# A sketched attention and a Fourier mixer in one kernel: q features made transposed on array tiles, rows s and s+544 folded, one written order

## The chip, the cores and the metric

The kernel runs on 1 core of one Trainium2 chip. The metric is device time in microseconds (us) from one launch to its end. The kernel before took 225.29 us, the median of three runs (224.28 to 231.45). The engines named here are TensorE (PE, with its weight loads as PEld), VectorE (DVE), ScalarE (ACT), GpSimd (POOL) and SyncE (SP, which only issues transfers here).

## The reference

```python
# q, k, v: (4, 4, 1088, 32) = (B, H, S, D); S1, S2: (8, 32); w_ch1 (128, 512); w_ch2 (512, 128)
def phi(x):                                   # 64 features for a row of 32
    a = einsum('rd,bhsd->bhsr', S1, x)
    b = einsum('rd,bhsd->bhsr', S2, x)
    return einsum('bhsi,bhsj->bhsij', a, b).reshape(*x.shape[:-1], 64)
kv  = einsum('bhsf,bhsd->bhfd', phi(k), v)
z   = sum(phi(k), axis=2)
x   = einsum('bhsf,bhfd->bhsd', phi(q), kv) / (einsum('bhsf,bhf->bhs', phi(q), z) + 1e-6)
x   = x.transpose(0, 2, 1, 3).reshape(B, S, 128)
u   = x + real(fft(fft(x, axis=1), axis=2))   # 1088 points along the rows, 128 along the columns
un  = (u - mean(u, -1)) / sqrt(var(u, -1) + 1e-6)
out = u + maximum(un @ w_ch1, 0) @ w_ch2      # (4, 1088, 128) float32
```

## The kernel before

Rows go in 9 tiles of a batch: 8 of 128 rows and one of 64. The type is float32 up to x and bfloat16 behind it. There are two halves.

**Attention, one batch at a time** (loop at L201). Twelve transfers bring q, k, v of the batch, in pieces of 128 bytes, half of q and k from ACT's queue, the rest from SP's (L208-L223). PE transposes q and k, tile by tile, with an identity (`ptr`, L255), ACT copies the result out (L261). `pab` (L269) multiplies the transposed rows by a block matrix of S1 and S2, which gives a and b of all four heads, row by row; ACT copies them (`ab`, L277), and DVE (two tiles of three) or POOL (the third) multiplies a by b into the 256 features of a row (`pp`, L282). So the features have rows in partitions. For k that is what the next product needs: `pkvz` (L292) sums features times [v, 1] over the 9 tiles, for two heads at a time, and ACT puts the two diagonal blocks into `kvz_sb` (L296, L297). For q it isn't: PE transposes the features once more (`pqpt`, L307), ACT copies them (`qpt_sb`, L315), `pnd` (L319) multiplies them by `kvz_sb`, and DVE divides, in three instructions for each tile and pair of heads (`recip` L327, `x_all` L329 and L336).

**Fourier and mixer.** A table of cosines and sines, 1088 rows by 545 columns, is made on DVE and ACT, tile by tile (`trig_tables`, L110 to L126), four tiles at the start and five behind batch 0. `emit_stage_a_main` (L154) multiplies x by it: for each batch 18 products of 512 columns and 18 of 33 (`za`, `za2`, `zbb`), which ACT copies into `zc`, `zs` and `zsn` (minus `zs`). Columns beyond 544 come from symmetry: DVE makes reversed copies (`zcr`, `zsr`, L379, L380). The last loop (L373 on) goes tile by tile: `pu` (L454 to L456) sums cosine part, sine part and x itself; DVE takes mean and variance, ACT the root, DVE normalises (`un`, L467), ACT copies u out (L471), PE transposes `un` (L475), and for four tiles at a time `ph` (L411), relu on ACT or DVE (L419, L422), `po` (L427), an addition of u on DVE (L435) and a store of 128 rows from SP's queue. 48 products of zeros (`wburst`, L383), 16 (`warm1`, L240) and 6 in float32 (`warm`, L230) are there to hold TensorE's clock and belong to no result.

**The order.** The code is written stage by stage. A scheduler of the framework places each engine's instructions, so products of different batches stand mixed on PE. Waits come from tile pools: a tile is handed out again when its last reader is done. In the last loop, tile 4 holds rows of both halves of the spectrum: for it the nested function `u_groups` writes output rows 0-31, 32-63 and 64-127 by three products each, group after group.

Of the kernel before, what the change touches and what calls it, by code (L numbers as in the profile page):

```python
# [42 lines left out]
def kernel(  # L43
# [35 lines left out]
    wdummy = const.tile([128, 512], BF16, name="wdummy")
    nc.gpsimd.memset(wdummy[:], 0.0)  # L80

    bias_negpi = const.tile([128, 1], FP32, name="bias_negpi")
    nc.vector.memset(bias_negpi[:], float(-np.pi))
    bias_eps = const.tile([128, 1], FP32, name="bias_eps")
    nc.vector.memset(bias_eps[:], 1e-6)

    s12 = const.tile([16, 32], FP32, name="s12")
    nc.sync.dma_start(s12[0:8, :], S1[:, :])
    nc.sync.dma_start(s12[8:16, :], S2[:, :])
    sblk = const.tile([128, 4, 16], FP32, name="sblk")  # L90
    nc.gpsimd.memset(sblk[:], 0.0)
    with tc.tile_pool(name="cps", bufs=1, space=bass.MemoryType.PSUM) as cps:
        ps12 = cps.tile([32, 16], FP32, name="ps12")
        nc.tensor.transpose(ps12[:, :], s12[:, :], ident_f[0:16, 0:16])
        for h in range(H):
            nc.vector.tensor_copy(sblk[32 * h : 32 * h + 32, h, :], ps12[:, :])

    kk_i = const.tile([128, KHALF], I32, name="kk_i")
    nc.gpsimd.iota(kk_i[:], pattern=[[1, KHALF]], base=0, channel_multiplier=0)
    kk_f = const.tile([128, KHALF], FP32, name="kk_f")  # L100
    nc.vector.tensor_copy(kk_f[:], kk_i[:])
    s_i = const.tile([128, NT], I32, name="s_i")
    nc.gpsimd.iota(s_i[:], pattern=[[128, NT]], base=0, channel_multiplier=1)
    s_f = const.tile([128, NT], FP32, name="s_f")
    nc.vector.tensor_copy(s_f[:], s_i[:])

    MAGIC = float(1.5 * (2 ** 23))
    TWOPI = float(2.0 * np.pi)

    def trig_tables(out_cos, out_sin, kq_ap, s_scalar_ap, ncols, tagsuf):  # L110
        x = const.tile([128, ncols], FP32, name="tx", tag="tx" + tagsuf)
        nc.vector.tensor_scalar(out=x[:], in0=kq_ap, scalar1=s_scalar_ap, scalar2=None,
                                op0=MULT)
        xc = const.tile([128, ncols], FP32, name="txc", tag="txc" + tagsuf)
        nc.vector.tensor_scalar(out=xc[:], in0=kq_ap, scalar1=s_scalar_ap, scalar2=0.25,
                                op0=MULT, op1=ADD)
        u = const.tile([128, ncols], FP32, name="tu", tag="tu" + tagsuf)
        nc.vector.tensor_scalar(out=u[:], in0=x[:], scalar1=MAGIC, scalar2=MAGIC,
                                op0=ADD, op1=SUB)
        uc = const.tile([128, ncols], FP32, name="tuc", tag="tuc" + tagsuf)  # L120
        nc.vector.tensor_scalar(out=uc[:], in0=xc[:], scalar1=MAGIC, scalar2=MAGIC,
                                op0=ADD, op1=SUB)
        nc.vector.tensor_tensor(out=x[:], in0=x[:], in1=u[:], op=SUB)
        nc.vector.tensor_tensor(out=xc[:], in0=xc[:], in1=uc[:], op=SUB)
        nc.scalar.activation(out=out_sin, in_=x[:], func=ACT.Sin, scale=TWOPI)
        nc.scalar.activation(out=out_cos, in_=xc[:], func=ACT.Sin, scale=TWOPI)  # L126

    kkq_d = const.tile([128, 128], FP32, name="kkq_d")
    nc.vector.tensor_scalar(out=kkq_d[:], in0=kk_f[:, 0:128], scalar1=1.0 / 128.0,
                            scalar2=None, op0=MULT)  # L130
    cd_b = const.tile([128, 128], BF16, name="cd_b")
    sd_b = const.tile([128, 128], BF16, name="sd_b")
    trig_tables(cd_b[:, :], sd_b[:, :], kkq_d[:, :], s_f[:, 0:1], 128, "d")

    kkq_s = const.tile([128, KHALF], FP32, name="kkq_s")
    nc.vector.tensor_scalar(out=kkq_s[:], in0=kk_f[:, :], scalar1=1.0 / S,
                            scalar2=None, op0=MULT)
    cst_b = const.tile([128, NT, KHALF], BF16, name="cst_b")
    sst_b = const.tile([128, NT, KHALF], BF16, name="sst_b")

    def emit_strig(t):
        trig_tables(cst_b[:, t, :], sst_b[:, t, :], kkq_s[:, :], s_f[:, t : t + 1],
                    KHALF, "s")

    for t in (0, 1, 2, 3):
        emit_strig(t)

    z_pool = ctx.enter_context(tc.tile_pool(name="zsb", bufs=B))
    ps_za = ctx.enter_context(tc.tile_pool(name="ps_za", bufs=1, space=bass.MemoryType.PSUM))
    zcs = [None] * B  # L150
    zss = [None] * B
    zsns = [None] * B

    def emit_stage_a_main(b):  # L154
        zc = z_pool.tile([128, KHALF], BF16, name="zc", tag="zc")
        zs = z_pool.tile([128, KHALF], BF16, name="zs", tag="zs")
        zsn = z_pool.tile([128, KHALF], BF16, name="zsn", tag="zsn")
        za = ps_za.tile([128, 512], FP32, name="za", tag="za")
        for t in range(NT):
            rows = rows_of_tile(t)  # L160
            nc.tensor.matmul(za[:, :], x_all[0:rows, b, t, :], cst_b[0:rows, t, 0:512],  # L161
                             start=(t == 0), stop=(t == NT - 1))
        nc.scalar.copy(zc[:, 0:512], za[:, :])
        za2 = ps_za.tile([128, 512], FP32, name="za2", tag="za")
        for t in range(NT):
            rows = rows_of_tile(t)
            nc.tensor.matmul(za2[:, :], x_all[0:rows, b, t, :], sst_b[0:rows, t, 0:512],
                             start=(t == 0), stop=(t == NT - 1))
        nc.scalar.copy(zs[:, 0:512], za2[:, :])
        nc.scalar.mul(zsn[:, 0:512], za2[:, :], -1.0)  # L170
        zbb = ps_za.tile([128, 512], FP32, name="zbb", tag="za")
        for t in range(NT):
            rows = rows_of_tile(t)
            nc.tensor.matmul(zbb[:, 0:33], x_all[0:rows, b, t, :], cst_b[0:rows, t, 512:KHALF],
                             start=(t == 0), stop=(t == NT - 1))
        for t in range(NT):
            rows = rows_of_tile(t)
            nc.tensor.matmul(zbb[:, 64:97], x_all[0:rows, b, t, :], sst_b[0:rows, t, 512:KHALF],
                             start=(t == 0), stop=(t == NT - 1))
        nc.scalar.copy(zc[:, 512:KHALF], zbb[:, 0:33])  # L180
        nc.scalar.copy(zs[:, 512:KHALF], zbb[:, 64:97])
        nc.scalar.mul(zsn[:, 512:KHALF], zbb[:, 64:97], -1.0)
        zcs[b] = zc
        zss[b] = zs
        zsns[b] = zsn

    with ExitStack() as aph:
        qin_pool = aph.enter_context(tc.tile_pool(name="qin", bufs=2))
        vin_pool = aph.enter_context(tc.tile_pool(name="vin", bufs=2))
# [11 lines left out]
        for b in range(B):  # L201
            if b >= 2:
                emit_stage_a_main(b - 2)
# [169 lines left out]
    for b in range(B):  # L373
# [139 lines left out]
```

## Time and profile before

| What | us |
|---|---|
| median of three runs | 225.29 (224.28 to 231.45) |
| the profiled execution: its span, first to last instruction | 224.3 |
| its own time (the lowest of the three runs, equal to the span) | 224.28 |
| ScalarE busy | 91.0 |
| GpSimd busy | 20.6 |
| mean granted TensorE clock | 0.794 of full |
| bytes moved | 10.04 MB in 61571 packets, 56560 of them under 512 B |

Busy times are sums over the whole span and overlap between engines. A matmul's own time holds its way through the array (0.22 us for 128 columns of bfloat16), so the distance from one start to the next, not the duration, tells what a product costs in a dense run. A float32 product is recorded as two matmuls with a weight load each.

### The profile page before, as it was taken

How to read it: one execution, taken by the hardware profiler on the slowest of the kernel's cores; microseconds unless marked ns; L12 is line 12 of the kernel's file. 1: busy time of each engine (PE TensorE's matmuls, PEld its weight loads, DVE VectorE, ACT ScalarE, POOL GpSimd, SP SyncE). 2: the span in 40 equal slices, each digit the busy share in tenths (PEclk: the TensorE clock that was granted, in tenths of full speed). 3: DMA queues.
4: the chain of work that ended last, by engine and by line, in shares of the span. 5: the costliest groups of instructions: out<-in, count | busy, mean ns of one | idle time of the engine just before them, and what ended most of it. 6: DMA issues, size and time to landing. Idle time of an engine off the chain costs nothing.

```text
span 224.3 us, 3592 instructions
## 1 busy us (share of the span) xinstructions
PE 185.6 (83%) x1157; PEld 128.2 (57%) x1157; DVE 138.3 (62%) x549; ACT 91.0 (41%) x290; POOL 20.6 (9%) x46
## 2 busy tenths in 40 slices
PE   0491599988848999999999999898999867868872
PEld 0231466878535978788879876553655433434431
DVE  2034897569995312668474456745387886877751
ACT  0030655357535321453252143514364464545440
POOL 3000131200031200132203100000000000000000
PEclk9997557999965555899995599959999996785555
DMA  8999995049800002400000000000011011111011
GB/s 102 142 130 194 164 151 56 4 73 155 87 0 0 0 0 43 65 0 3 1 0 0 3 1 1 3 0 0 21 29 53 26 38 42 35 34 33 24 36 41
DMA packets 61571, 10.04 MB, mean 45 GB/s; under 512 B 56560, under 2 KB 61424, under 8 KB 61552
## 3 DMA queue, kind: packets, MB, share of 16 engines
q1 hardware_dynamic: 42288, 6.95, 23.3%
q10 hardware_dynamic: 19264, 2.87, 10.6%
q8 instruction: 9, 0.15, 0.3%
q14 instruction: 10, 0.08, 0.1%
HBM read 7.58 MB, written 2.23 MB: 44 GB/s over the span
## 4 chain that ended last, share of the span: by engine, by line
PE 67%; DVE 12%; ACT 8%; ACTq 5%; DMA 4%; issue 2%; DVEq 0%
PE pkvz L292 9%; PE pab L269 9%; PE pnd L319 8%; PE pqpt L307 6%; ACTq L217 5%; PE wburst L383 5%; PE ph L411 5%; PE po L427 5%; DMA w_f<-in_moe_w_ch_dram 4%; PE za L161 4%; PE ptr L255 3%; ACT ht L419 2%; PE warm_621 L240 2%; PE pu L454 2%; PE put L475 2%
## 5 line engine op out<-in xcount | busy, mean ns | idle before, releaser
L327 DVE RECIPROCAL recip<-pnd 128x2 f32<-128x2 f32 (+1 forms) x72 | 12.0, 167 | 33.2 <-PE pnd L319 32.5
L319 PE MATMUL pnd<-kvz_sb,qpt_sb 128*128 128x66 f32 x144 | 29.8, 299 | 0.7 <-DVE recip L327 0.5
L319 PEld LDWEIGHTS pnd<-kvz_sb,qpt_sb 128*128 128x128 f32 x144 | 25.0, 215 | 7.2 <-issue 1.2
L282 DVE TENSOR_TENSOR pp<-ab 128x256 f32<-128x256 f32 (+1 forms) x48 | 21.2, 456 | 8.9 <-ACT ab L277 8.8
L292 PE MATMUL pkvz<-vin,pp 128*128 128x66 f32 x144 | 25.6, 317 | 0.0
L292 PEld LDWEIGHTS pkvz<-vin,pp 128*128 128x128 f32 x144 | 23.4, 232 | 2.0 <-issue 0.5
L427 PE MATMUL po<-w_b,ht 128*128 128x128 bf16 (+1 forms) x144 | 20.1, 251 | 4.3 <-DVE ot L435 3.6
L282 POOL TENSOR_TENSOR pp<-ab 128x256 f32<-128x256 f32 x24 | 17.2, 721 | 57.3 <-ACT ab L277 57.3
L307 PE MATMUL pqpt<-ident_f,pp 128*128 128x128 f32 (+1 forms) x72 | 19.1, 335 | 3.3 <-DVE pp L282 2.9
L427 PEld LDWEIGHTS <-ht 128*128 128x128 bf16 (+1 forms) x144 | 12.4, 111 | 15.3 <-issue 9.9
L277 ACT COPY ab<-pab 128x64 f32<-128x64 f32 (+1 forms) x72 | 13.9, 216 | 16.3 <-PE pab L269 15.4
L411 PE MATMUL ph<-unT,w_b 128*128 128x512 bf16 (+1 forms) x48 | 16.5, 387 | 4.4 <-ACT ht L419 2.2
L329 DVE TENSOR_SCALAR x_all<-pnd,recip 128x32 bf16<-128x32 f32 (+1 forms) x72 | 17.5, 242 | 0.4
L315 ACT COPY qpt_sb<-pqpt 128x512 f32<-128x512 f32 (+1 forms) x24 | 11.1, 463 | 15.7 <-PE pnd L319 9.5
L336 DVE TENSOR_SCALAR x_all<-pnd,recip 128x32 bf16<-128x32 f32 (+1 forms) x72 | 17.3, 240 | 0.0
L161 PE MATMUL za<-cst_b,x_all 128*128 128x512 bf16 (+1 forms) x36 | 16.2, 453 | 0.8 <-DVE x_all L336 0.8
L422 DVE TENSOR_SCALAR ht<-ph 128x512 bf16<-128x512 f32 (+1 forms) x24 | 12.8, 533 | 5.5 <-PE ph L411 4.9
L307 PEld LDWEIGHTS pqpt<-ident_f,pp 128*128 128x128 f32 (+1 forms) x72 | 12.3, 194 | 6.8 <-DVE pp L282 3.7
L435 DVE TENSOR_TENSOR ot<-po,u_sb 128x128 f32<-128x128 f32 (+1 forms) x36 | 10.3, 286 | 8.9 <-PE po L427 8.3
L269 PE MATMUL pab<-sblk,kT 128*128 128x64 f32 (+1 forms) x72 | 15.7, 340 | 0.0
L419 ACT ACTIVATE ht<-ph 128x512 bf16<-128x512 f32 (+1 forms) x24 | 11.3, 472 | 9.3 <-PE ph L411 9.2
L269 PEld LDWEIGHTS pab<-sblk,kT 128*128 128x128 f32 (+1 forms) x72 | 13.9, 252 | 1.7 <-ACT qpt_sb L315 0.4
(98 smaller groups left out, 325.8 us busy)
## 6 DMA issues: line engine op xcount, KB each, us to landing
vin<-in_v_dram SPq DMA_DIRECT2D x15, 144.0 KB, 4.0
out_dram<-ot SPq DMA_DIRECT2D x32, 64.0 KB, 1.5
qin<-in_q_dram SPq DMA_DIRECT2D x8, 144.0 KB, 5.8
kin<-in_k_dram SPq DMA_DIRECT2D x8, 144.0 KB, 4.1
qin<-in_q_dram ACTq DMA_DIRECT2D x7, 144.0 KB, 4.5
kin<-in_k_dram ACTq DMA_DIRECT2D x7, 144.0 KB, 6.3
w_f<-in_moe_w_ch_dram ACTq DMA_DIRECT2D x2, 256.0 KB, 6.7
qin<-in_q_dram ACTq DMA_DIRECT2D x1, 128.0 KB, 5.1
```

Of the source, the lines that this page charges most:

```text
L161: nc.tensor.matmul(za[:, :], x_all[0:rows, b, t, :], cst_b[0:rows, t, 0:512], start=(t == 0), stop=(t == NT - 1))
L269: nc.tensor.matmul(pab[0:rows, :, :], srcT[:, 128 * t : 128 * t + rows], sblk[:, :, :], start=True, stop=True,)
L277: nc.scalar.copy(ab[0:rows, :, :], pab[0:rows, :, :])
L282: eng.tensor_tensor(out=pp[0:rows, :, :, :], in0=in0, in1=in1, op=MULT)
L292: nc.tensor.matmul(pkvz[:, :, :], lhsT, rhs, start=(t == 0), stop=(t == NT - 1))
L307: nc.tensor.transpose(pqpt[:, col : col + rows], qp_tiles[t][0:rows, h0 : h0 + 2, :, :], ident_f[0:rows, 0:rows],)
L319: nc.tensor.matmul(pnd[0:rows, :, :], qpt_sb[:, c0 : c0 + rows], kvz_sb[:, :, :], start=True, stop=True,)
L329: nc.vector.tensor_scalar(out=x_all[0:rows, b, t, (h0 + 0) * D : (h0 + 1) * D], in0=pnd[0:rows, 0, 0:D], scalar1=recip[0:rows, 0:1], scala ...
L336: nc.vector.tensor_scalar(out=x_all[0:rows, b, t, (h0 + 1) * D : (h0 + 2) * D], in0=pnd[0:rows, 1, 0:D], scalar1=recip[0:rows, 1:2], scala ...
L411: nc.tensor.matmul(ph[:, 0:group_rows], w1_b[:, 128 * c : 128 * c + 128], unT[:, 0:group_rows], start=True, stop=True,)
L419: nc.scalar.activation(out=ht[:, c, 0:group_rows], in_=ph[:, 0:group_rows], func=ACT.Relu)
L427: nc.tensor.matmul(po[0:rows, :], ht[:, c, colbase : colbase + rows], w2_b[:, c, :], start=(c == 0), stop=(c == 3),)
```

## The change

All stages are written anew as named steps with an engine, a function that issues them, and a place in one long string that gives the issue order of all engines; a second string gives each step's PSUM bank. Nothing else orders the work: each engine takes its own steps in that order, with waits for what they read.

- **Layout.** Rows are dealt to partitions in runs. k and v: the 1088 rows of a head go to 32 partitions, 34 to each, of which 32 are loaded (k: one piece of 4 KB); v in pieces of 1 KB; q and out: partition p holds rows 4p to 4p+3 of the lower half (rows 0-511) or of the upper half (rows 544-1055), 512 B and 2 KB pieces. The 64 rows left over in each batch and head are loaded for all batches together (`kt_in`, `vt`, `qt_in`). All 37 loads and 16 stores are issued by SP.
- **k.** A DVE block transpose (32x32 blocks, `kT`) takes the place of `ptr`; `kpr` (8 products of 64 columns a batch) of `pab`; one ACT copy of 512 columns; a times b in four pieces of 512 elements, 11 of the 16 on POOL, 5 on DVE; `kv` as before, 18 products a batch.
- **q.** A DVE block transpose (`qT`), then 16 float32 products that use a 32-row by 64-column tile of the array each and give a (or b), already spread over the 64 features, with features in partitions; one ACT copy of a, one DVE product with b in PSUM. No second transpose. `pnd` as before, 18 products a batch; the division is three DVE instructions a batch.
- **Fourier.** x of row s and of row s+544 are added and subtracted (`eo`), so even columns need the sum and odd ones the difference: 5 instead of 9 tables, 273 columns of each kind, 20 products of 273 columns a batch. Even and odd are put together by one ACT copy, reversed copies go to POOL (6) and DVE (2).
- **Mixer.** Ten groups: 8 of 512 rows, 2 of 128. u is summed in one bank; mean is taken out of w1 by a matrix (`cen`) rather than out of u, so `un` is u times 1/sd; `po` adds onto u in u's own bank, and one copy and one store of 256 KB end the group.
- **Gone:** the zero bursts but one of 12 at the start, `ptr`, `pqpt`, `qpt_sb`, `u_sb`, `zsn`, `bn_aggr`.

The core of the diff (before's code is taken out whole):

```diff
+    def kproj(use, src, tiles, n):
+        for t in range(tiles):
+            nc.tensor.matmul(ps(use, 64 * t, [[1, 64]], 0, n), view(src, n * t, [[1, n]]), T("sblk")[:],
+                             start=True, stop=True)
+    def kprod(engine, ab, kp, lo, hi, n):
+        tt(engine, view(kp, F * lo, [[F, hi - lo], [R, R], [1, R]], 0, n),
+           view(ab, 16 * lo, [[16, hi - lo], [1, R], [0, R]], 0, n),
+           view(ab, 16 * lo + R, [[16, hi - lo], [0, R], [1, R]], 0, n), ALU.mult)
+    def kT(b):
+        nc.vector.transpose(view(T(f"kT{b % 2}"), 0, [[1, 4], [128, 8], [4, 32]]), T(f"k_in{b % 2}")[:])
+    def vcopy(b):
+        nc.gpsimd.tensor_copy(view(T(f"v{b}"), 0, [[33, H], [33 * H, 8], [1, D]]),
+                              view(T(f"v_in{b % 2}"), 0, [[8 * D, H], [D, 8], [1, D]]))
+    def kv(b):
+        for pr in range(2):
+            for t in range(9):
...
+                nc.tensor.matmul(ps(f"kv{b}", 66 * pr, [[1, 66]]), kp, v, start=(t == 0), stop=(t == 8))
+    def qfeat(b, pr):
+        for g in range(4):
+            for h in range(2):
+                for w, src in enumerate(("sa", "sb")):
+                    nc.tensor.matmul(
+                        ps(f"q{b}.{pr}", 512 * g + 256 * w, [[1, 256]], 64 * h, 64),
+                        view(T(src), 0, [[1, F]], 32 * g, 32),
+                        view(T(f"qT{b % 2}"), 128 * (2 * pr + h), [[512, 2], [1, 128]], 32 * g, 32),
+                        start=True, stop=True, tile_position=(32 * g, 64 * h), skip_group_check=True)
+    def qa(b, pr):
+        nc.scalar.copy(T(f"qa{pr}")[:], ps(f"q{b}.{pr}", 0, [[512, 4], [1, 256]]))
+    def qp(b, pr):
+        nc.vector.tensor_tensor(
...
+            in0=ps(f"q{b}.{pr}", 256, [[512, 4], [32, 8], [1, 32]]),
+            in1=view(T(f"qa{pr}"), 0, [[256, 4], [32, 8], [1, 32]]), op=ALU.mult)
+    def xx(b):
+        nc.vector.tensor_tensor(out=view(T(f"x{b}"), 0, [[384, 3], [32, 12], [1, 32]]),
+                                in0=ps(f"nd{b}", 0, [[512, 3], [33, 12], [1, 32]]),
+                                in1=view(T(f"den{b % 2}"), 0, [[12, 3], [1, 12], [0, 32]]), op=ALU.mult)
+    def srow(b, trig):
+        for c in range(2):
+            for t in range(5):
+                w = T(f"eo{b % 2}")[:, c, t, :] if t < 4 else T("xl")[:, b, :]
+                m = T("tab")[:, t, trig, NK * c:NK * c + NK]
+                nc.tensor.matmul(ps(f"z{trig}{b}", 512 * c, [[1, NK]]), w, m, start=(t == 0), stop=(t == 4))
+    def mix(b, half):
+        u = f"u{b}.{half}"
+        nc.tensor.matmul(ps(u, 0, [[1, 512]]), T("idb")[:], view(T(f"x{b}"), 512 * half, [[1, 512]]),
+                         start=True, stop=False, skip_group_check=True)
+        for t in range(4):
+            for trig in range(2):
+                w = T("cd")[:] if trig == 0 else T("sd")[:, half, :]
+                nc.tensor.matmul(ps(u, 128 * t, [[1, 128]]), zcol(b, trig, half, t, 4, 128), w, start=False, stop=True,
+                                 skip_group_check=True)
+    def po(u, g, n):
+        for t in range(n):
+            for c in range(4):
+                nc.tensor.matmul(ps(u, 128 * t, [[1, 128]]), T(f"ht{g % 2}")[:, c, 128 * t:128 * t + 128],
+                                 T("w2b")[:, c, :], start=False, stop=True, skip_group_check=True)
...
+    with tc.manual_schedule():
+        for name in order:
+            steps[name].emit()
```

The order string, from its start to the last `pnd` (`ld_` load, `t_` tables, `c_` constants; `kp`, `vc`, `zr`, `eo`: products, copies and folds; `bn`, `var`, `sd`, `un`, `tr`, `ut`, `ph`, `rl`, `po`, `fin`, `out`: the mixer's steps of a group in that order):

```
c_iota ld_v0.2 c_bias c_wz warm ld_kt c_v12 ld_k0 c_mask ld_qt c_rows t_turn1 ld_q0.1 ld_s kt_T t_turn0 t_ph1 ld_q1.1
ld_q0.0 t_sin1 t_pm1 t_ph0 t_cos1 c_kvz ld_v0.0 c_eye16 ld_v0.1 c_v10 t_pm0 ld_q1.0 t_sin0 kT0 t_cos0 c_cen c_ktp
ld_k1 ld_v0.3 c_vt ld_k2 qt_T qT0.1 s_t ld_vt t_turn4 s_use qt_f qT1.1 ld_v1.0 kt_pr t_ph4 c_xl qt_a t_turn3 ld_v1.2
kpr0 kt_ab qT0.0 ld_v1.3 qt_p t_sin4 ld_v1.1 ld_q3.0 qf0.0 kab0 c_v13 kt_p1 c_v11 c_idb ld_q3.1 kp0.1 qa0.0 qf0.1
kt_p0 ld_w1 qT1.0 ld_q2.1 qa0.1 kp0.2 ld_q2.0 qp0.0 ld_w2 qf1.1 qp0.1 kp0.3 kT1 qa1.1 kp0.0 qf1.0 ld_k3 vc0 qa1.0
qp1.1 ld_v2.3 kpr1 qp1.0 t_turn2 ld_v2.2 kT2 kv0 ld_v2.1 kab1 kp1.0 ld_v2.0 kp1.2 kvz0 kp1.1 t_ph2 kpr2 kp1.3 kab2
pnd0 t_pm2 vc1 kp2.3 t_cos2 t_pm4 ld_v3.1 kp2.0 t_sin2 qT3.0 kv1 ld_v3.3 t_cos4 den0 d_turn x0 ld_v3.2 ld_v3.0 kp2.1
kvz1 w1c w1b pnd1 t_ph3 eo0.1 qT2.1 t_sin3 t_pm3 t_cos3 xl0 eo0.0 qT2.0 sS0 den1 w2b sC0 x1 zS0 zrS0 qf2.1 zC0 d_ph
d_pm eo1.0 eo1.1 d_trig kp2.2 qf2.0 qa2.1 zrC0 kT3 qa2.0 qp2.1 xl1 mix1 qp2.0 vc2 mix0 bn1 sC1 bn0 kv2 zC1 vc3 var0
sd0 var1 un0 zrC1 sd1 sS1 un1 kvz2 tr0 kpr3 zS1 qT3.1 ut0 zrS1 tr1 pnd2 ut1 kab3 kp3.3 kp3.2 den2 ph1.1 mix3 kp3.1 x2
rl1.1 eo2.1 ph1.0 ph0.1 bn3 mix2 rl1.0 xl2 var3 rl0.1 eo2.0 kp3.0 ph0.0 po1 bn2 rl0.0 sS2 var2 sd3 fin1 un3 sd2 zS2
po0 out1 qf3.1 zrS2 fin0 qa3.1 kv3 out0 un2 qp3.1 kvz3 tr2 qf3.0 ut2 ph2.1 qa3.0 rl2.1 qp3.0 ph2.0 rl2.0 tr3 pnd3 ut3
...
```

More of the change, by code (lines that the diff above doesn't have):

```diff
@@ new lines, with __init__, view @@
+ACT = mybir.ActivationFunctionType
+B, H, S, D, R = 4, 4, 1088, 32, 8
+DM = H * D
+HID = 4 * DM
+HALF = S // 2
+F = R * R
+ROWS = S // 32
+LAST = HALF - 512
+NK = HALF // 2 + 1
+MAGIC = float(1.5 * 2 ** 23)
+PI = float(np.pi)
+class Step:
+    def __init__(self, name, engine, emit, reads, writes, psum):
+        self.name, self.engine, self.emit = name, engine, emit
+        self.reads, self.writes, self.psum = reads.split(), writes.split(), psum.split()
+def view(t, offset, dims, p0=0, n=128):
+    a = t[:]
+    step = a.ap[0][0]
+    return bass.AP(tensor=a.tensor, offset=a.offset + p0 * step + offset,
+                   ap=[[step, n]] + [list(d) for d in dims])
@@ L87 @@
[L87 to L96, printed above, removed]
@@ L128 @@
[L128 to L137, printed above, removed]
@@ L151 @@
[L151 to L185, printed above, removed]
@@ new lines @@
+    x = {"q": q, "k": k, "v": v, "S1": S1, "S2": S2, "w1": moe_w_ch1, "w2": moe_w_ch2, "out": out}
+    steps = {s.name: s for s in program(nc, made.__getitem__, x, BANK.__getitem__)}
+    order = ORDER.split()
+    assert sorted(order) == sorted(steps)
+    with tc.manual_schedule():
+        for name in order:
+            steps[name].emit()
+KP_ENGINE = {
+    "1.2": "DVE", "1.3": "DVE", "2.2": "DVE", "2.3": "DVE", "3.2": "DVE", "t0": "DVE", "t1": "DVE",
+}
+EO_ENGINE = {
+    "0.1": "POOL", "1.0": "POOL", "2.1": "POOL", "3.1": "POOL",
+}
```

770 lines of the change are left out of this document (407 added, 363 removed), and 5 rows, old and new, of the table MIX_ENGINE.

## The prediction

> **What bounds the kernel now.** First the page's busy times, slices and chain, to see which engine sets the end.
>
> ```profile
> PE 185.6 (83%) x1157; PEld 128.2 (57%) x1157; DVE 138.3 (62%) x549; ACT 91.0 (41%) x290; POOL 20.6 (9%) x46
> ...
> PE   0491599988848999999999999898999867868872
> ...
> PEclk9997557999965555899995599959999996785555
> ...
> PE 67%; DVE 12%; ACT 8%; ACTq 5%; DMA 4%; issue 2%; DVEq 0%
> ```
>
> TensorE holds two thirds of the chain, and is busy in slices where its clock stands at half. Second, the sums by stretch, to see what that clock is worth (columns: stretch, its length, busy us and count of PE, PEld, DVE, ACT, POOL, then clock, DMA share, GB/s):
>
> ```profile
> 64.00:76.00 12.00, 9.88 (x41) 7.78 (x42) 7.82 (x18) 6.17 (x19) 2.00 (x3) 0.50 0.00 0
> 76.00:88.00 12.00, 12.00 (x51) 9.92 (x51) 2.50 (x12) 2.53 (x10) 0.79 (x2) 0.50 0.00 0
> 92.00:116.00 24.00, 23.67 (x190) 19.68 (x189) 16.42 (x75) 11.62 (x44) 6.08 (x10) 1.00 0.01 2
> ```
>
> Equally dense streams of much the same products: 51 in 12 us at half clock, 190 in 24 us at full. The clock fell after a stretch with PE half idle (60 to 64 us, 1.93 of 4 busy) and stayed low for 25 us of dense work. Third, the chain in order of time, for prices (start, us, what):
>
> ```profile
> 44.53 1.79 PE pkvz L292 x16
> ...
> 82.65 2.99 PE pkvz L292 x14
> ...
> 155.48 2.05 PE za_1785 L167 x9
> ```
>
> A float32 product of 66 columns is two records: 0.112 us each at full clock (1.79 / 16), 0.214 at half. A bfloat16 product of 512 columns is 0.228.
>
> Fourth, the timeline where u's tile 4 is written: three products for output rows 0-31, then three for rows 32-63, in the code's order.
>
> ```profile
> 171.83 0.23 PE L454 MATMUL pu<-cd_b,zc 128*32 128x128 bf16 x1
> 171.84 0.23 PE L454 MATMUL pu<-cd_b,zcr 128*32 128x128 bf16 x1
> 171.89 0.22 PE L455 MATMUL pu<-sd_b,zsn 128*32 128x128 bf16 x1
> 171.90 0.22 PE L455 MATMUL pu<-sd_b,zsr 128*32 128x128 bf16 x1
> 171.95 0.23 PE L456 MATMUL pu<-x_all,ident_b 128*32 128x128 bf16 x2
> ```
>
> One tile's products start 0.06 apart (171.83, 171.89, 171.95); the other tile's (zcr, zsr), issued behind all of them, start 0.01 after. Two column tiles of the array run side by side, and a waiting product of one doesn't hold the next tile's.
>
> Fifth, groups for POOL and the small DVE work:
>
> ```profile
> L282 POOL TENSOR_TENSOR pp<-ab 128x256 f32<-128x256 f32 x24 | 17.2, 721 | 57.3 <-ACT ab L277 57.3
> L327 DVE RECIPROCAL recip<-pnd 128x2 f32<-128x2 f32 (+1 forms) x72 | 12.0, 167 | 33.2 <-PE pnd L319 32.5
> L459 DVE BATCH_NORM_STATS2 stats<-pu 128x6 f32<-128x128 f32 x32 | 9.3, 292 | 6.0 <-PE pu L456 5.5
> ```
>
> **The change part by part, PE at full clock.** Gone: 72 transposes `ptr` of q and k and 72 `pqpt` at 0.11 (0.44 for four `pqpt` at 48.81) = 16 us; 36 q `pab` at 0.224 = 8; the zero bursts, 48 + 16 at 0.228 = 15; in the Fourier rows 72 of 512 columns and 72 of 33 (0.052 each, nine `zbb` in 0.47) = 16.4 + 3.7 become 80 of 273 (0.12 each) = 9.7. `pkvz` and `pnd` stay as they are: 144 products x 0.224 = 32.3.
>
> Added: the q features. Eight steps `qf` of 16 float32 products with 256 columns, 32 records. The float32 `warm` records of 512 columns start 0.45 apart (eight in 3.74, the last taking 0.59), so 0.22 for 256. All 32 one after another: 7.0 us. All eight tiles at once: four records a tile, 0.9, plus 32 starts 0.01 apart, 1.2. The row it is nearest to is the pair at 171.83, so I take 1.2; that row shows two column tiles, not four row groups, and this is the largest unknown.
> [...]
>
> The rest of PE: `kpr` 32 x 0.224 = 7.2, mixer sums 8 x 0.7 + 1, transposes 34 x 0.06, `ph` 34 x 0.228, `po` 136 x 0.06, `w1c` 0.9: with the above some 75, plus 10 for q and 1 for its left-over rows. So 86 us of PE.
>
> Other engines, from rows. ACT: 22 passes of 1024 columns at 1.0 (0.587 for 512, 0.216 for 64), 34 of 512 to 546 at 0.6, small ones 6: about 48. DVE: `bn` 34 x 0.29 = 10, `qp` 8 x 1.2, division 4 x 1.7, block transposes 8 x 0.6 and 4 x 1.2, tables 6, `kp` 7 x 0.6, `var` and `un` 14, copies and relus 9: about 70, under 122. A block transpose stands in no row: between 0.29 (`zcr`, 544 columns of bfloat16) and twice the float32 product (0.64 for 545), so 0.3 to 1.2 for 512; I take the product. POOL: 11 `kp` x 1.44, tables 7 to 17, copies, folds and memsets 27: about 50.
> [...]
>
> **The sum, in three stages** read from the order string.
>
> *Start to `kv0`.* POOL is last. Its queue ahead: 0.7 start, iotas 1.1, a wait for DVE's seven small instructions 1.1 (0.16 each), four `t_turn` of two passes over 546 at 0.58 (the 545-column iota; 4.7), memsets and masks 5.1 (0.53 for 512 columns), four `kp0` of 512 at 2 x 0.721 (5.8), `vc0` 1.1: 20 us. Loads: 2.9 MB stand in SP's queue up to v's last piece for batch 0, 15 us at the 194 GB/s that 128-byte pieces reached at best in the page's slices, so hidden; at the 102 of the first slice, 28, which would show. PE beside it: S at about 11, then 5 + 4 x 1.2, done at 21. Bounds: 17 if one-input passes go faster, 29 if they cost as `pp` does (2.8 ns a column).
>
> *`kv0` to `pnd3`.* PE's queue in order: four `kv` and `pnd` 32.3, `kpr2`, `kpr3` 3.6, five Fourier steps 6.1, four `qf` 4.8, `mix` 2.8, `tr` 1.0, six `ph` halves 2.7, two `po` 1.9, `w1c` 0.9 = 56. In that time DVE has some 40 and POOL 25, ACT 25, so PE leads; handovers that nothing covers (`kvz` by ACT twice 0.18 before each `pnd`, `zC` and `zrC` before `mix`) 3.
>
> *Behind `pnd3`.* PE still has 19.8 queued; the last batch's chain (division 1.7, fold 0.6, Fourier 2.4, copies 1.1, sums 1.4, `bn` to `un` 2.9, `tr` to `rl` 2.7, `po` 1.0, copy 0.6, store 1.5) is 16. So 20 and the last copy and store, 22.
>
> 20 + 59 + 22 = 101 at full clock. The clock: in 62 to 152 us before, where the same float32 products ran, it was 0.76 on average with PE as dense; 56 / 0.76 adds 18, and 3 show of the tail at 0.78. **122 us.** What it costs: DVE and POOL hinder each other when both read SBUF (`tuc` took 0.86 at 62.62 beside a POOL `pp`, 0.44 at 21.57 alone); DVE has the room, POOL would lose 1 or 2. The span equals the lowest of the three runs, and the median is 0.4% above it; I add nothing.
>
> **Rivals.**
> 1. Row groups don't run side by side, only column pairs: `qf` 3.8, +2.6 x 4 in the first stage, where PE then passes POOL (+11), and x 4 at 0.76 later (+14): 147. For it: no row with four row groups; a product with 64 weight rows at 157 us (157.14) began 0.31 behind the one before, not 0.22. [...]
> 2. Tiles one at a time at full clock, so that the layout does not do what it says: 7.0 a step, 176. Against: 171.83.
> 3. POOL's one-input passes cost as `pp`: `kv0` at 29, 131.
> 4. The clock stays full: 101 to 104. Against: four half-clock stretches with dense PE in this trace.
> 5. Slower: products in 32-row tiles leave TensorE's clock at half to the end and run one after another. Then a step is 14, eight 113, the rest 150, with the start and end over 280. The point from which it decides: 230 is reached at half clock and 7.7 a step, that is fewer than two tiles at a time. Against: the full clock from 92 to 116 under float32 products, and the pair at 171.83.
>
> **The numbers.** Forecast 0.67 (104 to 135 with the clock's and POOL's bounds), column pairs 0.09, strict order 0.06, one at a time 0.03, POOL 0.10, full clock 0.03, slower 0.02. The range 103 to 148 leaves out strict order, one at a time, slower and the edge of full clock and pairs, under 0.2. A measurement of this kernel tells about 2% from no change. Faster by more: 0.97; within: 0.01 (one at a time, part of it at half clock); slower: 0.02.
>
> **What would show it.** A `qf` step about 1.2 us from first to last start at full clock (3.8, 5.5 or 7.0 for the rivals); the first `kv` at 20 us with POOL's `vc0` its releaser (29 by rival 3); the last `pnd` ended near 100 us, with PE over half of the chain; mean clock about 0.8. It is wrong if DVE or ACT, not PE, leads between `kv0` and `pnd3`, if loads release `kv0`, or if PE waits there for more than 3 us.

## The result, and the profile after

The changed kernel took 140.37 us (median of four runs, 139.77 to 141.71); the kernel before, run beside it, took 225.32. The ratio is 0.624, with a 95% interval from 0.619 to 0.629. The forecast was 122, with a range of 103 to 148. The profiled execution took 141.71, its span is 139.9. Here and there in the experiments one run of a kernel is some per cent slower than the others, at a lower mean clock; the ratios leave such runs out.

The page of the changed kernel: busy times, TensorE's and POOL's slices, the clock, the chain's shares.

```profile
PE 118.2 (85%) x1045; PEld 99.5 (71%) x1045; DVE 79.0 (56%) x178; ACT 51.3 (37%) x84; POOL 43.7 (31%) x70
...
PE   6508998499999999999996999988995998988640
...
PEclk9955555955555555555569999999999999999996
...
PE 69%; DVE 14%; ACT 8%; issue 3%; DMA 2%; SPq 0%; ACTq 0%; DVEq 0%
```

TensorE still holds two thirds of the chain. The clock is at half from the third slice to the twenty-first, with one full slice between, although TensorE is nearly always busy there. The sums by stretch (columns as in the prediction):

```profile
6.00:8.00 2.00, 0.00 (x0) 0.00 (x0) 1.97 (x4) 1.85 (x4) 1.74 (x8) 0.86 1.22 212
...
26.00:27.00 1.00, 0.33 (x16) 0.00 (x0) 1.00 (x2) 0.70 (x2) 0.00 (x0) 1.00 0.00 0
27.00:28.00 1.00, 0.00 (x0) 0.00 (x0) 1.00 (x2) 0.51 (x1) 0.00 (x0) 0.97 0.00 0
...
32.00:40.00 8.00, 8.00 (x39) 8.00 (x39) 4.89 (x4) 0.83 (x3) 4.54 (x3) 0.50 0.13 35
40.00:64.00 24.00, 24.00 (x109) 22.97 (x108) 8.09 (x11) 4.84 (x10) 6.08 (x7) 0.50 0.04 12
...
68.00:72.00 4.00, 4.00 (x19) 2.55 (x17) 3.83 (x8) 0.78 (x1) 1.09 (x2) 0.50 0.01 2
72.00:80.00 8.00, 6.64 (x109) 5.50 (x107) 6.55 (x19) 4.65 (x8) 4.48 (x6) 0.98 0.01 2
```

The clock falls twice, each time behind a pause of TensorE: at about 7.5 us (nothing to do since 5.4) and at 28 (0.33 us of work in two). From 28 to 68 TensorE is busy all the time, PEld nearly so, and the clock stays at half. It rises only at 72, behind more than 4 us of Fourier products, where PEld is no longer full. The chain in order of time shows what that costs:

```profile
11.11 2.95 PE ps L348 x32
14.05 4.65 PE ps L262 x24
18.71 4.10 PE ps L325 x63
22.83 1.02 ACT t_qa__119 L332
23.88 1.22 DVE t_qp__120 L336
25.10 2.02 DVE t_kT__107 L280
27.12 1.06 DVE t_qp__121 L336
28.22 3.68 PE ps L262 x16
31.90 7.68 PE ps L295 x36
...
78.65 3.97 PE ps L295 x36
```

L295 is `kv`, L370 `pnd`. The 36 records of a `kv` take 7.68 at half clock and 3.97 at full. The pause before 28.22 is DVE's: `kpr1` (L262) writes the bank that `qp1.1` still reads, and `qp1.1` stands behind `kT1`, a block transpose of 1024 elements that takes 2.0 us.

The timeline where one q step runs at full clock:

```profile
103.09 0.73 PE L325 MATMUL ps<-t_qT__109,t_sa 32*64 32x256 f32 x16
103.57 0.68 PE L325 MATMUL ps<-t_qT__109,t_sb 32*64 32x256 f32 x16
```

All 32 records lie within 1.2 us; the first starts at 103.1 and the last at 103.9, 0.79 apart.

The end of POOL's part in the first stage (timeline of POOL):

```profile
19.41 4.14 POOL L74 TENSOR_TENSOR t_kp__112<-t_ab__110 128x512 f32<-128x512 f32 x4 [5.01 <-ACT t_ab__110 L306]
23.50 1.05 POOL L283 COPY t_v__114<-t_v_in__101 128x1024 f32<-128x1024 f32 x1
```

POOL was done at 24.55, 7.3 us before the first `kv` began at 31.90. It was not last.

### The profile page after: what moved, and what is told of

It is laid out like the page before. It is cut to its first block, busy times and chain, and to the rows that moved or that the text cites. A ratio compares the mean times of both kernels' runs of the same rounds, so it can differ in the third digit from the quotient of the medians.

```text
span 139.9 us, 2609 instructions
## 1 busy us (share of the span) xinstructions
PE 118.2 (85%) x1045; PEld 99.5 (71%) x1045; DVE 79.0 (56%) x178; ACT 51.3 (37%) x84; POOL 43.7 (31%) x70
## 4 chain that ended last, share of the span: by engine, by line
PE 69%; DVE 14%; ACT 8%; issue 3%; DMA 2%; SPq 0%; ACTq 0%; DVEq 0%
PE ps L295 17%; PE ps L370 17%; PE ps L262 10%; PE ps L397 8%; PE ps L325 5%; PE ps L482 3%; PE ps L468 3%; DMA t_kt_in<-in_k_dram 2%; PE ps L348 2%; ACT t_ht__148 L475 2%; PE ps L417 2%; DVE t_qp__120 L336 2%; ACT t_ht__149 L475 1%; ACT t_qa__119 L332 1%; DVE t_kT__107 L280 1%
## 5 line engine op out<-in xcount | busy, mean ns | idle before, releaser
L370 PEld LDWEIGHTS ps<-t_kvz,t_qp__121 128*128 128x128 f32 x64 | 10.7, 263 | 1.0 <-ACT t_kvz L67 0.5
L74 POOL TENSOR_TENSOR t_kp__113<-t_ab__111 128x512 f32<-128x512 f32 x5 | 6.7, 1361 | 13.6 <-ACT t_ab__111 L306 13.6
L370 PE MATMUL ps<-t_kvz,t_qp__120 128*128 128x66 f32 x64 | 10.8, 348 | 0.0
L370 PE MATMUL ps<-t_kvz,t_qp__121 128*128 128x66 f32 x64 | 10.7, 346 | 0.0
L370 PEld LDWEIGHTS ps<-t_kvz,t_qp__120 128*128 128x128 f32 x64 | 10.6, 262 | 0.0
L475 ACT ACTIVATE t_ht__149<-ps 128x1024 bf16<-128x1024 f32 x7 | 7.1, 1023 | 9.2 <-PE ps L468 9.2
L74 POOL TENSOR_TENSOR t_kp__112<-t_ab__110 128x512 f32<-128x512 f32 x6 | 6.8, 1149 | 11.6 <-ACT t_ab__110 L306 11.6
L475 ACT ACTIVATE t_ht__148<-ps 128x1024 bf16<-128x1024 f32 (+1 forms) x8 | 7.7, 973 | 1.3 <-PE ps L468 1.3
L397 PE MATMUL ps<-t_tab,t_eo__128 128*128 128x273 bf16 x32 | 6.9, 358 | 0.5 <-ACT t_sm__141 L449 0.5
L262 PE MATMUL ps<-t_sblk,t_kT__106 128*128 128x64 f32 x32 | 7.3, 423 | 0.0
L295 PE MATMUL ps<-t_v__114,t_kp__112 128*128 128x66 f32 x32 | 7.2, 421 | 0.0
L295 PE MATMUL ps<-t_v__115,t_kp__113 128*128 128x66 f32 x32 | 7.2, 421 | 0.0
L262 PE MATMUL ps<-t_sblk,t_kT__107 128*128 128x64 f32 x32 | 5.6, 350 | 1.9 <-DVE t_qp__121 L336 1.9
L262 PEld LDWEIGHTS ps<-t_sblk,t_kT__106 128*128 128x128 f32 x32 | 7.0, 332 | 0.1
L295 PEld LDWEIGHTS ps<-t_v__114,t_kp__112 128*128 128x128 f32 x32 | 7.1, 333 | 0.0
L295 PEld LDWEIGHTS ps<-t_v__115,t_kp__113 128*128 128x128 f32 x32 | 7.1, 333 | 0.0
L262 PEld LDWEIGHTS ps<-t_sblk,t_kT__107 128*128 128x128 f32 x32 | 5.4, 261 | 2.3 <-DVE t_qp__121 L336 2.3
```

The costliest lines, as they stand in the source:

```text
L74: (nc.vector if engine == DVE else nc.gpsimd).tensor_tensor(out=out, in0=in0, in1=in1, op=op)
L262: nc.tensor.matmul(ps(use, 64 * t, [[1, 64]], 0, n), view(src, n * t, [[1, n]]), T("sblk")[:], start=True, stop=True)
L295: nc.tensor.matmul(ps(f"kv{b}", 66 * pr, [[1, 66]]), kp, v, start=(t == 0), stop=(t == 8))
L370: nc.tensor.matmul(ps(f"nd{b}", 512 * (s // 3) + 132 * (s % 3) + 66 * pr, [[1, 66]]), w, view(T("kvz"), 132 * b + 66 * pr, [[1, 66]]), sta ...
L397: nc.tensor.matmul(ps(f"z{trig}{b}", 512 * c, [[1, NK]]), w, m, start=(t == 0), stop=(t == 4))
L475: nc.scalar.activation(out=out, in_=in_, func=ACT.Relu)
```

## The experiments

All are edits of the changed kernel. `warm2` and `warm3` are new steps of TensorE that multiply zeros (bfloat16, 512 columns) into a free bank. Theory A is that pauses like the two above (3.9 us from 5.4 to 9.2, 1.9 ahead of 28.22) drop the clock, and that the float32 stream, at half from 28 to 68, can't raise it again. Its rivals are that the float32 stream itself lowers the clock, whatever stands ahead of it, and that the time hangs on DVE or POOL instead.

**A burst in the pause**, ten products in bank 5.

```diff
-qp1.1 ld_v2.3 kpr1 qp1.0
+qp1.1 ld_v2.3 warm2 kpr1 qp1.0
```

> The changed kernel with 10 bfloat16 products of zeros (512 columns) on PE ahead of kpr1; nothing else is altered. Theory A (a pause of PE of 1.9 us before kpr1 lets the clock fall, and the float32 stream behind it, bound by weight loads, can't lift it for 44 us): the burst takes at most 4.3 us at half clock, the clock is 1.00 within 4 us of its start and stays there, the 44 us from kpr1 to the second Fourier step become about 22, and the time is about 122 us. Theory B (the float32 stream itself holds the clock at half, whatever came before): the clock falls back within a few us, and the time is about 144.

Measured: 126.72 us (126.45 to 126.79), ratio 0.572 [0.565, 0.578]. Sums by stretch of this run:

```profile
28.00:32.00 4.00, 3.82 (x26) 2.73 (x25) 3.15 (x3) 0.00 (x0) 0.00 (x0) 1.00 0.82 260
32.00:40.00 8.00, 8.00 (x75) 8.00 (x73) 6.14 (x6) 2.78 (x6) 5.75 (x4) 1.00 0.11 29
40.00:52.00 12.00, 12.00 (x104) 11.32 (x104) 7.70 (x13) 2.95 (x6) 4.86 (x7) 1.00 0.10 28
...
56.00:60.00 4.00, 0.58 (x8) 0.48 (x8) 4.00 (x4) 1.53 (x2) 2.26 (x2) 1.00 0.00 0
60.00:62.00 2.00, 2.00 (x17) 1.52 (x15) 1.70 (x7) 0.00 (x0) 0.00 (x0) 0.52 0.00 0
```

2.3 us of zeros that compute nothing take 13.7 us off. The same float32 stream that stayed at half after 28 us runs at full here, 75 records in 8 us instead of 39. So here the stream keeps the clock that it finds. The rest to the 122 of theory A was lost in a second pause: from 55.2 to 59.4 TensorE waits for DVE, and the clock falls behind it.

**A burst in the middle of the half-clock stream**, with no pause ahead of it (ten products, bank 4).

```diff
+warm2 kv1
-kv1
```

> The changed kernel with the 10 zero products ahead of kv1, in the middle of the 44 us at half clock, where PE has no pause before or behind. Theory A (what the clock follows is how densely the array is fed: the float32 stream, bound by weight loads, feeds it about half the time and neither lifts a low clock nor drops a high one): the burst takes 3.5 to 4.3 us, the clock is 1.00 behind it, the 21 us from kv1 to the end of the second Fourier step become 11, and the time is 140 + 4 - 10.5 = about 134 us. Theory A' (only a pause ahead of it matters, the clock can't be lifted while the stream runs): +4, 144 us.

Measured: 137.57 (137.49 to 142.67), ratio 0.614 [0.611, 0.616]. Sums by stretch:

```profile
40.00:48.00 8.00, 8.00 (x39) 8.00 (x39) 2.54 (x3) 2.53 (x4) 3.44 (x4) 0.50 0.00 1
48.00:52.00 4.00, 3.78 (x16) 2.13 (x17) 3.19 (x6) 0.00 (x0) 1.18 (x1) 0.66 0.00 0
52.00:60.00 8.00, 8.00 (x68) 7.52 (x68) 2.35 (x4) 2.20 (x5) 1.46 (x3) 1.00 0.01 2
...
66.00:68.00 2.00, 0.00 (x0) 0.00 (x0) 2.00 (x3) 1.32 (x2) 2.00 (x2) 0.94 0.00 0
68.00:72.00 4.00, 2.57 (x19) 2.17 (x20) 3.21 (x8) 0.00 (x0) 0.06 (x1) 0.50 0.02 4
```

Full busy time alone doesn't raise the clock here (0.50 from 40 to 48 us, TensorE busy 8.00 of 8.00); with ten products of zeros, from 48.7 on, it is at 1.00 from 52. Part is given back: earlier work on TensorE meets DVE's chain at 65, and the pause drops the clock once more.

What sets the float32 stream apart is a weight load for every 66 columns: PEld is busy 8.00 of 8.00 us beside it, and 2.55 of 4 ahead of the rise at 72 in the changed kernel. But a full PEld is not what holds the clock down: in the kernel before it stayed at half from 76 to 88 us with PEld busy 9.92 of 12, and in the row-group experiment below from 18 to 46 with PEld busy 17.50 of 28. That the feeding of the array's columns counts, and not type or length, is thus a guess; these runs don't tell them apart. The "half the time" of the expectation is an estimate: at the 0.45 us between starts of float32 records of 512 columns before, 66 columns are 0.06 of the 0.112 us of a record.

**The same burst where the clock is full.**

```diff
-kpr3
+warm2 kpr3
```

> The changed kernel with the same 10 zero products ahead of kpr3, at some 84 us, where the clock is full already. All theories of the clock: the burst is pure cost, 10 x 0.22 = 2.2 us on PE's queue, 141 to 143 us. Rival (such a burst helps by where it delays or spreads the other engines, not by the clock): less than 140.

Measured: 142.1 (141.86 to 144.09), ratio 0.633 [0.631, 0.636]: about 2 us more, the price of the zeros. No other help of the zeros shows where the clock is full already.

**A shorter pause.**

```diff
-kt_p0 ld_w1 qT1.0 ld_q2.1
+kt_p0 ld_w1 qT1.0 kT1 ld_q2.1
...
-kp0.3 kT1 qa1.1
+kp0.3 qa1.1
```

> The changed kernel with the DVE block transpose kT1 moved in the order from between qp0.1 and qp1.1 to ahead of qp0.0, where DVE idles 4.5 us; no work is added or left out. Theory A: qp1.1 ends some 2 us earlier, kpr1 follows the q products with a pause under 1 us, the clock that the q products had lifted at 24.5 us stays at 1.00, and the time is 140 - 2 - 22 = about 116 us. Theory B: the clock falls all the same, 138 us. Theory C (the loss at the start is waiting for DVE, not the clock): only the 2 us, 138 us too, but with the half clock from 28 us on untouched.

Measured: 139.58, 137.12, 124.64 and 139.47, too far apart for a ratio. In the profiled run (139.58) the pause is 1.2 us instead of 1.9, and the clock still falls at about 28.9. One of four runs gained 15 us; it wasn't profiled, but its mean clock is 0.905 where the others have 0.79 to 0.83. Nothing in the program differs between these runs, so behind a pause of this size the clock falls in some and not in others.

**More zeros at the start.**

```diff
-warmup(12)
+warmup(28)
```

> The changed kernel with 28 instead of 12 products of zeros at the very start, which fill PE's pause between 5.4 and 9 us. Theory A: the clock is 1.00 from 11 us to 26, the left-over q step takes 1.3 instead of 2.95 us, kpr0 1.8 instead of 3.7, a q step 0.95 instead of 2.05, so kv0 could start 4 to 6 us earlier; but PE then waits longer for DVE and POOL ahead of kpr1, so the clock may fall there again, and the time is 134 to 136 in that case and about 114 if it does not. Theory B: 136, with half clock from kpr1 on in any case.

Measured: 138.94 (137.21 to 140.57), ratio 0.621 [0.601, 0.642]. A miss: TensorE does nothing but S from 9.1 to 11.2, behind the zeros, and the clock is at half again from 12 on.

**The start at full clock**: the first experiment, 28 zeros at the start, and nine more behind `s_t`.

```diff
-qT0.1 s_t ld_vt
+qT0.1 s_t warm3 ld_vt
```

> The kernel of e1_burst with PE's pause at the start filled too: 28 zero products instead of 12 at the very start, and 9 more behind the transpose of S, until the q products can begin at 11 us. [...] Rival (POOL's products kp0 and v's copy release kv0 at about 25 whatever PE does, rival 3 of the prediction): kv0 starts at 28 or later, and the time is 124 to 125.

Measured: 123.35 (122.74 to 124.19), ratio 0.550 [0.547, 0.554]. The clock is at 1.00 to about 56 us. The first `kv` begins at 28.17, 4.06 earlier than in the first experiment: the left-over rows begin 1.15 later, behind the added zeros, and what took 2.95, 4.65 and 4.10 from there takes 1.58, 2.54 and 2.3. The time is 0.65 below the 124 to 125 expected, with `kv0` at 28 or later as expected, but POOL is not the cause. What stands between TensorE's second q step and `kv0` is as long as in the first experiment (9.5 us), and 5.4 of it is DVE's work (`qp` twice, `kT1`, `qp1.1`); the zeros and `kpr1` take most of the rest. POOL's `vc0` ended at 22.18.

**Row groups left out.** All 16 products of a q step read the first 32 rows, so that all use row group 0. Three of the four row blocks of q are not computed; the count and size of the products are unchanged.

```diff
-view(T(src), 0, [[1, F]], 32 * g, 32),
-view(T(f"qT{b % 2}"), 128 * (2 * pr + h), [[512, 2], [1, 128]], 32 * g, 32),
-start=True, stop=True, tile_position=(32 * g, 64 * h), skip_group_check=True)
+view(T(src), 0, [[1, F]], 0, 32),
+view(T(f"qT{b % 2}"), 128 * (2 * pr + h), [[512, 2], [1, 128]], 0, 32),
+start=True, stop=True, tile_position=(0, 64 * h), skip_group_check=True)
```

> The changed kernel with all four row groups of a q step taken from rows 0-31 of q and S, so that only two column tiles of the array are in use (3 of 4 row blocks of q are left out, their place is filled from the first). Theory (all eight tiles run side by side): a step goes from 0.93 us to 3.4 at full clock and from 2.05 to 6.9 at half, so four at half clock cost 19 and four at full 10, and the time is 160 to 170, less what the denser PE gains in clock. Rival (only column pairs overlap, row groups do not): a step stays as it is and the time stays at 140.

Measured: 180.11 (178.8 to 181.42), ratio 0.813 [0.778, 0.847]. Chain of this kernel, four q steps at half clock and one at full:

```profile
18.67 27.55 PE ps L325 x128
...
118.24 3.65 PE ps L325 x32
```

A step takes 3.65 here against 1.25 with four row groups, and from start to start 3.35 against 0.79. So all eight tiles run side by side. The time is above the expected 160 to 170 because the clock fell twice more, at about 89 and 123 us (page of this kernel, slices of 4.4 us):

```profile
PE   7459999999999999999999999889999799998850
...
PEclk9965555555555555569955899998555555999996
```

The last `kv`, q step and `pnd` run at half for it: 6.86, 7.09 and 7.68 us, where a `kv` and a `pnd` take 4.16 and 4.04 in the changed kernel and a step of this kind 3.65 at full clock: 9.8 more together. TensorE had no pause ahead of either fall: the profile has it busy from 80 to 96 us and from 116 to 128 without a gap, and each fall comes 4 to 5 us after a q step on two column tiles began. The kernel before has such a fall too:

```profile
116.00:118.00 2.00, 2.00 (x23) 1.57 (x22) 1.07 (x6) 1.30 (x9) 0.16 (x2) 1.00 0.00 0
118.00:128.00 10.00, 10.00 (x48) 9.37 (x49) 4.14 (x20) 2.47 (x11) 2.50 (x4) 0.51 0.01 2
```

So theory A is incomplete. A pause can drop the clock, as the first experiment shows, but streams with float32 products have also lost it with TensorE busy all the time. What sets these apart from the stream that kept it for 24 us in the first experiment is not shown.

**Both pauses mended**: the full start, the shorter pause, and DVE's work that isn't urgent moved from behind the division of batch 1 to ahead of it.

```diff
-sS0 den1 w2b sC0 x1 zS0 zrS0 qf2.1 zC0 d_ph d_pm eo1.0 eo1.1 d_trig kp2.2 qf2.0 qa2.1 zrC0 kT3
+sS0 d_ph d_pm kp2.2 kT3 den1 w2b sC0 x1 zS0 zrS0 qf2.1 zC0 eo1.0 eo1.1 d_trig qf2.0 qa2.1 zrC0
```

> The kernel of e5_start_full with kT1 on DVE ahead of qp0.0, and four DVE steps (d_ph, d_pm, kp2.2, kT3, together 3.5 us) moved from between x1 and qp2.1 to ahead of den1, where DVE waits for PE. No work is added or left out against e5. Theory: in e1 PE stood still from 55.2 to 59.4 us behind this DVE chain and lost its clock for 3 us; now mix1 follows the q steps within 1.5 us: 4 + 1.5 us less than e5, and 1 to 2 less ahead of kpr1, so about 115 us. Rival (DVE's order is not what PE waits for there, the banks are): no more than 1 us less than e5.

Measured: 118.28 (117.41 to 121.4), ratio 0.526 [0.522, 0.530], between the two expectations. The clock is full throughout (mean 0.998 in the profiled run). About 4 us of DVE's work put *ahead* of the division took the pause away: it fills time in which DVE waited for `pnd1` (3.35 us in the kernel without this edit), instead of standing between `x1` and the Fourier products.

**The folds on DVE.**

```diff
-EO_ENGINE = {"0.1": "POOL", "1.0": "POOL", "2.1": "POOL", "3.1": "POOL"}
+EO_ENGINE = {}
```

> This is e6_all with the four folds eo0.1, eo1.0, eo2.1 and eo3.1 on VectorE instead of GpSimd. Theory C (VectorE and GpSimd hinder each other while both read SBUF): a fold costs VectorE 0.42 us alone (three of after's took 0.41 to 0.42), against 1.06 for the one that ran beside a GpSimd fold, a 128x1 instruction of L444 that took 1.02 beside one instead of 0.16, and 1.15 on GpSimd itself. VectorE then has 4 x 0.42 more and at least 0.64 + 0.86 less, and each batch's Fourier products start 0.3 to 0.7 earlier: 117.0 us, 1 to 1.5 less than e6_all, with no instruction of the small sort above 0.3 us in the last batch. Rival: VectorE is the engine that TensorE waits for in every batch, so 4 x 0.42 more of it comes straight on top: 119 to 120 us.

Measured: 116.45 (116.27 to 120.9), ratio 0.519 [0.516, 0.521]. Timeline of DVE behind `x3`, first in the kernel with the folds on POOL:

```profile
91.04 1.01 DVE L449 SCALAR_TENSOR_TENSOR t_sm__142<-t_sm__142 128x1 f32<-128x1 f32 x1
91.97 0.41 DVE L74 TENSOR_TENSOR t_eo__129<-t_x__127 128x512 bf16<-128x512 bf16 x1
```

POOL's fold in it, from its own timeline:

```profile
90.88 1.15 POOL L74 TENSOR_TENSOR t_eo__129<-t_x__127 128x512 bf16<-128x512 bf16 x1
```

And DVE with all folds on it:

```profile
89.36 0.16 DVE L449 SCALAR_TENSOR_TENSOR t_sm__142<-t_sm__142 128x1 f32<-128x1 f32 x1
89.43 0.76 DVE L74 TENSOR_TENSOR t_eo__129<-t_x__127 128x512 bf16<-128x512 bf16 x2
```

One element a partition takes 1.01 us beside POOL's fold and ends with it (92.05 against 92.03); with POOL free it takes 0.16, and two folds take less than DVE's wait and one fold before. The medians lie 1.8 apart, and 1.4 (117.78 and 116.38) without the highest run of each kernel. In the profiled runs 88.8 us pass from the start of `kv0` to the end of the span with the folds on POOL and 87.2 with them on DVE; the rest of their difference is the start, where the 28 zeros took 9.18 us in one run and 8.25 in the other. So the folds are worth about 1.5, as expected.

**Without the middle zeros**, three kernels: the mended one without `warm2`; the same with all folds on DVE; and that with 24 zeros at the start.

```diff
-qp1.1 ld_v2.3 warm2 kpr1 qp1.0
+qp1.1 ld_v2.3 kpr1 qp1.0
```

> This is e6_all with its ten products of zeros ahead of kpr1 taken out, so that kT1's earlier place alone has to keep TensorE's pause ahead of kpr1 short. [...] Theory A' (the window ahead of kpr1 is still half empty, as in e2_kT1_early, where it fell in three runs of four): the clock falls at about 27 us, and kv0, pnd0, kv1 and pnd1 take 7.6 instead of 4.0 each, 14 us more: 131 us, or runs that lie at both values.

Measured: 116.25 (116.05 to 116.72), ratio 0.517 [0.515, 0.520]. The clock of the profiled run is at 1.00 from 20 to 28 us without the zeros, and the time is 2.0 below that of the mended kernel with them.

> e9_no_mid_burst and e10_fold_dve in one: no zeros ahead of kpr1, all folds on VectorE. The two lie in different stretches (24 to 26 us, and behind x0, x1, x2 and x3), so if both are what they were taken for the gains add: 118.28 - 2.03 - 1.83 = 114.4 us. Rival: the fold's gain in e10 came from an earlier start of the same stretch that e9 moves as well, and they overlap: 115.5 to 116.3.

Measured: 114.80, 119.89, 132.0, 132.29, 133.46 and 133.7. No ratio is given for them.

> e11_both with 24 instead of 28 zeros at the start. In e9 the 28 end at 10.1 and the left-over q rows begin at 12.3, after nine more zeros behind S; in the kernel of the change, with 12 zeros, they began at 11.1. If TensorE's zeros hold the left-over rows back, four fewer (0.23 each) start all of it 0.9 earlier: 113.5 us. If what the left-over rows wait for is their own transfer or transpose, the same as e11; and if the window between the zeros' end and S at 9.2 is now empty enough, the clock falls at about 12 us and the first stage takes 4 to 8 us more: 118 to 122.

Measured: 114.34, 118.58, 118.81, 132.28, 133.4 and 133.51, no ratio. In its profiled run the left-over rows began at 11.43, as in the kernel with 28 zeros (11.44), and in both where the nine zeros behind S end: the 24 zeros took 7.98 us in this run and the 28 took 7.99 in that one, where they came faster from the fourth microsecond on (16 starts from 4 to 7 us against 12). So the pair doesn't tell whether zeros hold the rows back. The first kernel does: there the 28 took 8.83, DVE's copy of S was done at 11.38, and the rows began at 12.29, as the nine zeros ended. Zeros held them back by 0.9.

Sums by stretch of the second of the three (a run of 132.0):

```profile
22.00:23.00 1.00, 0.00 (x0) 0.00 (x0) 1.00 (x1) 0.96 (x1) 0.80 (x2) 1.00 1.04 293
23.00:24.00 1.00, 0.86 (x8) 0.86 (x8) 1.00 (x2) 0.00 (x0) 0.00 (x0) 1.00 0.97 361
...
25.00:26.00 1.00, 1.00 (x9) 1.00 (x8) 1.00 (x2) 0.58 (x1) 0.16 (x1) 0.68 0.70 226
26.00:27.00 1.00, 1.00 (x7) 1.00 (x6) 1.00 (x2) 0.00 (x0) 1.00 (x2) 0.50 0.08 23
```

The pause ahead of `kpr1` is back, and the clock falls 2 us behind its end. The first kernel has the same pause (1.29 us in both profiled runs) and its four runs lie within 0.7 us, at mean clocks of 0.989 to 0.992. Whether chip, chance or the placing decides, these runs don't tell; what happens in the runs at 118 to 120 wasn't profiled. The lowest times, 114.3 and 114.8, are thus not what these two kernels take as a rule. Of the versions that hold the clock with zeros in the pause, the one with all folds on DVE is the best: 116.45, against 140.37 for the change as it was made.

## Why the prediction was right, and which step was off

The time is in the stated range, and the mechanism of the likeliest case is the one that the traces show from `kv0` on. But the time is 18 us above the forecast, and above 104 to 135, the bounds of that case; the part of the range above that took in column pairs (147), which didn't come true. That 140 falls inside it is in part luck. Stage by stage, against the span (the profiled execution's 1.8 us outside its span come on top; the prediction added nothing there, since before showed none):

| Stage | predicted | the change | without the middle zeros (116.36) |
|---|---|---|---|
| start to `kv0` | 20 | 31.9 | 25.8 |
| `kv0` to `pnd3` | 59 + 18 for the clock | 79.4 | 60.1 |
| behind `pnd3` | 22 + 3 for the clock | 28.6 | 28.7 |

The last column is the first kernel of the last experiment, whose clock is full nearly throughout.

- **Start to `kv0`: the step that failed, by 11.9 us.** "POOL is last" was wrong. POOL took 4.1 us for `kp0` where 5.8 was forecast, and waited for ACT. Last was a chain that goes from engine to engine. With the clock full it is still there, as this chain of the kernel without the middle zeros shows:

```profile
14.52 0.75 DVE t_qtp L362 x2
15.28 1.19 DVE t_ktp L74 x2
16.47 0.62 DVE t_qT__109 L322
17.09 1.97 DVE t_kT__107 L284
19.06 1.06 DVE t_qp__120 L340
20.16 1.32 PE ps L329 x32
21.51 1.02 ACT t_qa__119 L336
22.55 1.24 DVE t_qp__121 L340
23.83 2.00 PE ps L266 x16
25.83 4.02 PE ps L299 x36
```

  DVE's 70 us were weighed against the whole time, "under 122", and called room; in this stage DVE works without a gap from 14.5 to 20.1 and hands over one by one. That is 5.8 of the 11.9 (25.8 against 20). The other 6.1 are mostly clock: the start at full clock took 4.1 off by itself (the kernel of the last column also has `kT1` earlier, and left-over rows that begin 1.2 later, most of it behind its zeros). The sum had no term for it: the prediction priced this stage at full speed, although an idle TensorE, as between its zeros and S here, is just what it had read ahead of the fall at 60 to 64 us before (1.93 of 4 us busy).
- **TensorE's work: right.** The kernel with all folds on DVE ran at a mean clock of 1.00 with 99.4 us of TensorE busy, 8.25 and 4.43 of it zeros. That leaves 86.7, where 86 was forecast.
- **`kv0` to `pnd3`: right in both terms, the second in part by luck.** With the clock full the stretch takes 60.1 (59 forecast): 56.2 of TensorE busy (56) and 3.9 of waits (3). So the clock cost 79.4 - 60.1 = 19.3 (18 forecast). The average of 0.76 stood for something else, though: half until 72 us, full behind it. Where the clock falls, and for how long, the prediction didn't derive; with ten zeros ahead of `kpr1`, the first experiment, the same stage took 64.1.
- **Behind `pnd3`: 3.6 low.** TensorE's work was right (20.1 us busy, 19.8 forecast) and the clock was full, so the 3 for it were not needed. What was missed is 3.6 us of gaps from 111.3 to 134.95 (0.9 of it the 128x1 instruction behind POOL's fold) and 4.95 us behind TensorE's last product, where 2.1 were forecast: a copy, and then four stores of 16 KB that SP issues one by one (135.75 to 137.5).
- **The q step: right, and a little too dear.** 0.79 from first to last start where 1.2 was taken (1.25 in the chain, with the time of the last product), the right end of bounds from 0.9 to 7.0. The pair of column tiles at 171.83 before carried over to eight tiles. The rivals of column pairs and one tile at a time fall with it; the row-group experiment shows what pairs cost, 3.35 a step. The 5.5 us among the signs, for strict order, no run shows: at 171.83 before a later product starts ahead of an earlier one, and the step took 0.79.
- **The other rivals.** POOL's passes didn't decide: POOL was busy 43.7 us, 50 forecast. That `kv0` began at 31.9, near the 29 of this rival, has another cause. The full clock (101 to 104) was refused rightly for the change, and even 116 is not 101, for the DVE chain and the tail stay. The rival on the slower side needed half clock to the end and fewer than two tiles at a time; the first held to 72 us, the second never.
- **The signs it named.** True: the q step, TensorE over half of the chain (69%), a mean clock of 0.77 to 0.80. Missed: `kv0` at 20 behind `vc0` (31.9, behind `kpr1`) and the end of `pnd3` near 100 (111.3). One of its signs of being wrong, waits of TensorE over 3 us between `kv0` and `pnd3`, came up narrowly: they are 3.9.
- **Sizes of rows that before didn't show.** A block transpose of 512 elements took 0.69 (0.6 taken) and one of 1024 2.0 (1.2 taken), 3.9 us more for the twelve. DVE came to 79 us in place of 70, ACT to 51 in place of 48.

## What to carry to other kernels

Count an engine's room stage by stage, not over the span: here an engine busy 56% of the time stood in the chain of the first stage and made the pause of 1.9 us behind which TensorE's clock fell to half. Where a stream of float32 products with a weight load each is to run fast, look at the microseconds ahead of it: if TensorE pauses there, zeros in the pause can be worth more than they cost (2.3 us of them took 13.7 off), and the same zeros where the clock is full cost their own time (about 2 us). A dense stream isn't safe either: products on two column tiles lost the clock without a pause (at about 89 and 123 us of the row-group experiment). A pause that one run in four survives (1.2 us, 124.64 against 137 to 140) isn't mended; repeat the run before a gain is counted.

## What the hardware showed that was not expected

Beside the clock under the float32 stream and the instruction held up by POOL's fold:

- A block transpose doesn't scale with its size: 0.45 us for 256 elements, 0.69 for 512, 2.0 for 1024. The last also writes its result in another order (steps of 128 and 4 elements); size and order weren't told apart.
- Loads reached 334 GB/s in the page's slices, where 194 was the most before, with pieces of 512 B to 4 KB in place of 128 B.
